# A fused attention and mixer kernel: batch 0's last casts off GpSimd, its mixed rows ahead of the turns, a mask and one v load moved

## The chip, the cores and the metric

The kernel runs on one core of one Trainium2 chip. The metric is the time of one execution on the device, in microseconds (us). A trace of one execution lies beside the times; its engines are TensorE (PE, with its weight loads as PEld), VectorE (DVE), ScalarE (ACT), GpSimd (POOL) and SyncE (SP).

## What is computed

Eight batches go through sparse attention and then through a mixer in tokens and channels. Cut to what matters:

```python
# q, k, v: (8 batches, 8 heads, 576 rows, 64); 8 global rows for all batches
scores = q @ k.T / 8
mask   = |i - j| <= 32  or  i is global  or  j is global
attn   = softmax(where(mask, scores, -1e9))
x      = concat_heads(attn @ v)                      # (8, 576, 512)
h      = relu(x.T @ w_tok1) @ w_tok2                 # 576 -> 256 -> 576
u      = x + h.T
out    = u + relu(u @ w_ch1) @ w_ch2                 # 512 -> 1536 -> 512
```

## The kernel before

**The tiles.** A batch's 576 rows are five tiles of 128 (tau, the last of 64 rows). Heads go in pairs p = 0 to 3. Loads bring q and k in f32 into `lq`, `lk` (rows 0 to 511) and `lr` (the 64 rest rows of both). These three buffers exist once, so a load for the next batch waits until the last one is cast. `cast_qk` (L365) makes f16 copies `qk` and `rn`. The rows must then be turned so that head elements lie on partitions. Batches 0 to 2 are turned on TensorE (`T`, `TR`) and copied out of PSUM into `qT`, `kT` by `TE` (L454) and `TR` (L458). Batches from 3 on are turned by DMA on SP's queue (`turns`, L752) and put in order by DVE (`order_*`).

**The attention.** `S_` makes the scores of a head pair in two PSUM tiles, and ACT takes their exponentials into `e_all` in three instructions (L494, L511, L516). For batch 0 the mask is added in the matmuls; for the others `SM` (L525) multiplies by `bandm` on DVE. `SM` also copies the columns of the global rows into `eg`. The scores of global rows go through `GK` (L540): two exponentials into `lf`, then a product with the 0/1 mask `mf`. `OG` (L562) multiplies `eg` by v. `PV` (L578) multiplies `e_all` by v, adds the product of `lf` with `OG`'s result `rf`, and divides by the sums into `x16`.

**The mixer.** `M1` and `M2` are the token part, its sums being `u16`. u is turned into `uT` by `M3` (L679), four DMA transposes on SP's queue (and one for the last 64 rows of two batches). `M4` (12 groups of four matmuls, relu by ACT or DVE) and `M5` are the channel part. Batch 0 has its own form: `M23_first` (L655) adds x and h for one tile, and `M3_first` (L671) turns that tile on TensorE and copies it out.

**The order** is written out by hand; each engine runs its instructions in the order of the program. After a prologue for batch 0 (L888 to L997), `period(b)` (L757) puts the channel part of batch b, held as a list `dense` from which `d(k)` takes k pieces, between the attention and the token part of batch b + 1. In period 0 (`n == 1`) these come one after another on GpSimd: `load_v16(2)` (L818, five DMAs that bring v of batch 2 and cast it to f16 into `vsh[0]`), four casts of k of batch 2, and `gather(1)` (four indirect DMAs). In the same period SP issues `load(3)` (q and k of batch 3; its lk waits for those four casts), the stores of batch 0 and the transposes of u of batch 1. In period 1 (`n == 2`) GpSimd casts batch 3: `casts(3)` (L808), first the rest rows, then eight pieces of q and k, then issues `load(4)` and `load_v16(3)`.

**PSUM.** Three buffers rotate under `s` (turned pieces, scores, `GK`, `OG`, `PV`, `pu`), two under `m` (`M4`, `M5` and others). A tile waits until the buffer three (or two) allocations back is read out.

The lines of the prologue that the change touches are L918 to L942 (casts, pads, turns and scores of batch 0) and L986 to L992 (mixed rows and turns of u of batch 0). In them `cast0(ti, p, eng)` casts head pair p of q (ti 0) or k (ti 1) of batch 0, `e_pads(i)` clears a part of `e_all` with a DVE memset (L190), `G0(p)` makes the global rows' part and `castv` casts v of batch 0 on GpSimd (L411).

Of the kernel before, what the change touches and what calls it, by code (L numbers as in the profile page):

```python
# [15 lines left out]
P = 128  # L16
NT = 5
# [9 lines left out]
def kernel(  # L27
# [12 lines left out]
    nc = tc.nc  # L40
# [148 lines left out]
    def e_pads(i):  # L189
        nc.vector.memset(  # L190
            (
                e_all[:, 2 * i : 2 * i + 2, :, 0:64] if i < NP else e_all[:, :, 0, 64:P] if i == NP
                else e_all[:, :, NT - 1, 64 + GW + P :]
            ), 0.0,
        )

    def row_numbers():
        nc.vector.tensor_scalar(out=idx_i, in0=bc_f, scalar1=hb, scalar2=gpp, op0=ALU.add, op1=ALU.add)
# [57 lines left out]
    def pads(i, eng):  # L256
        eng.memset(vsh[i][0:WIN, 0], 0.0)
        eng.memset(vsh[i][P - WIN : P, NT - 1], 0.0)
        eng.memset(vsh[i][:, :, :, D + 1 : VW], 0.0)
        eng.memset(vsh[i][:, :, :, D : D + 1], 1.0)  # L260
        eng.memset(x16s[i][LAST - 64 * i : P - 64 * i, NT - 1, :], 0.0)
# [4 lines left out]
    mf = const.tile([P, NT * P], F16)  # L266
# [88 lines left out]
    st = [dict() for _ in range(B)]  # L355

    def load_v16(b, c0=0, c1=NT):
        for c in range(c0, c1):
            r0, r1, j0 = vrows(c)
            nc.gpsimd.dma_start(  # L360
                out=vsh[b % 2][r0:r1, c, :, 0:D],
                in_=v[b, :, j0 : j0 + (r1 - r0), :].rearrange("h p d -> p h d"),
            )
# [9 lines left out]
    def casts(b, eng):  # L373
        return [lambda: cast_qk(b, 0, None, eng)] + [
            lambda ti=ti, p=p: cast_qk(b, ti, p, eng) for p in range(NP) for ti in range(2)
        ]
# [58 lines left out]
    def T(b, p):  # L435
        pT = pss([P, 2, 4 * P], F16, name=f"pT_{b}_{p}")
        for ti in range(2):
            for t in range(4):
                nc.tensor.transpose(out=pT[:, ti, P * t : P * t + P], in_=qk[:, ti, p, t], identity=ident)
        st[b]["pT", p] = pT  # L440
# [13 lines left out]
    def TE(b, p, copy):  # L454
        TE_q(b, p, copy)
        TE_k(b, p, copy)

    def TR(b, copy):  # L458
        pr = pss([P, NP, P], F16, name=f"pr_{b}")
        for p in range(NP):  # L460
            nc.tensor.transpose(out=pr[:, p], in_=rn[:, p], identity=ident)
        copy(out=qTs[b % 2][:, :, NT - 1, GW : GW + LAST], in_=pr[:, :, 0:LAST])
        copy(out=kTs[b % 2][:, :, WIN + 512 : WIN + S], in_=pr[:, :, LAST:P])
# [58 lines left out]
    def S_all(b, p):  # L522
        return S_(b, p, 0) + S_(b, p, 1)
# [16 lines left out]
    def GK(b):  # L540
        s = st[b]
        ps = pss([P, 2, 512], name=f"gk_{b}")
        for p in range(NP):
            o = ps[32 * p : 32 * p + 32]
            qv = qTs[b % 2][:, p, :, GW:QS]
            w = kgz[:, b, p, :]
            nc.tensor.matmul(o[:, 0, 0:384], lhsT=w, rhs=qv[:, 0:3], start=True, stop=True)
            nc.tensor.matmul(o[:, 1, 0:256], lhsT=w, rhs=qv[:, 3:5], start=True, stop=True)
        lf = mb.tile([P, NT * P], F16, tag="lf", name=f"lf_{b}")
        nc.scalar.activation(out=lf[:, 0:384], in_=ps[:, 0, 0:384], func=AF.Exp, scale=scale)  # L550
        nc.scalar.activation(out=lf[:, 384:640], in_=ps[:, 1, 0:256], func=AF.Exp, scale=scale)
        s["lf"] = lf
        if b > 0:
            nc.vector.tensor_mul(out=lf, in0=lf, in1=mf)
        else:
            lf_mask(0, 384)

    def lf_mask(x0, x1):
        lf = st[0]["lf"]
        nc.vector.tensor_mul(out=lf[:, x0:x1], in0=lf[:, x0:x1], in1=mf[:, x0:x1])  # L560

    def OG(b):  # L562
# [178 lines left out]
    def d(k, keep=0):  # L741
        for _ in range(k):
            if len(dense) > keep:
                dense.pop(0)()
# [12 lines left out]
    def period(b):  # L757
        n, m = b + 1, b + 2
        odd = b % 2
        dense.extend(lambda j=j: M4(b, j) for j in range(NJ))  # L760
        if odd:
            dense.extend(lambda j=j: M4l(b, j) for j in range(3))
        dense.extend(lambda t=t, i=i: M5(b, t, i) for t in range(4 + odd) for i in range(2))
        if n == B:
            d(len(dense))
            return
        tail = len(dense) - (23 if odd else 20) - 2 * odd
        keep = 3 if n == 1 else 0

        def scores(p, k):  # L770

            es = S_all(n, p)
            es[0]()
            es[1]()
            relu_on_dve[0] = n > 2 and p == 3
            d(1)
            relu_on_dve[0] = False
            es[2]()
            if n < 3 and p < 2:
                T(n, p + 2)  # L780
            d(1 + k)
            if n > 2 and p < 2:
                order(n, p + 2)
            if n < 3 and p < 2:
                TE(n, p + 2, dve)
            SM(n, p)

        if n == 1:
            d(1)
            gather_t(0)  # L790
            globals_(1)
            T(1, 1)
            TE_q(1, 1, act)
            TE_k(1, 1, dve)
            masks_d()
            pads(1, nc.vector)
            d(1)
            M2(0, 2)
        if n > 2:
            load(n + 2)  # L800
        scores(0, tail > 5)
        scores(1, max(tail - 4 - (tail > 5), 0))
        scores(2, 0)
        GK(n)
        if n > 2 and m < B:
            turns(m)
        if n == 2:
            for c in casts(3, nc.gpsimd.tensor_copy):  # L808
                c()
            load(4)  # L810
            turns(3)
        d(1)
        scores(3, 0)
        if n == 1:
            c2 = casts(2, nc.scalar.copy)
            for c in c2[0:1] + c2[1::2]:
                c()
            load_v16(2)  # L818
            for p in range(NP):
                cast_qk(2, 1, p, nc.gpsimd.tensor_copy)  # L820
            load(3, nc.sync)
            gather(1)
        d(1)
        OG(n)
        d(1)
        if n == 3:
            gather_t(1)
        fill = [order_rest, lambda i: order_k(i, 0), lambda i: order_q(i, 0), lambda i: order_k(i, 1), lambda i: order_q(i, 1)]
        lag = 2 if n == 1 else 1
        for tau in range(NT):  # L830
            PV(n, tau)
            if lag <= tau < 3 + lag:
                M1(n, tau - lag)
            if n > 2 and m < B:
                fill[tau](m)
            if n == 2 and tau > 2:
                fill[tau - 3](m)
            if tau < 4 and n > 1:
                d(1)
        if m < B:  # L840
            globals_(m)
        M1(n, 3)
        if n == 2:
            order_q(3, 0)
        d(1 if n == 1 else len(dense) - (8 + 2 * odd), keep)
        M1(n, 4)
        d(1, keep)
        if 2 < m < B:
            load_v16(m)
        M2(n, 0)  # L850
        M3(n, 0)
        M2(n, 1)
        M3(n, 1)
        M2(n, 2)
        if n % 2:
            M3(n, 2)
        if 1 < n < B - 2:
            for c in casts(n + 2, nc.scalar.copy):
                c()
        if n == 1:  # L860
            d(1, keep)
            T(2, 0)
            TE(2, 0, act)
            TR(2, dve)
            T(2, 1)
            d(1, keep)
            TE(2, 1, dve)
        else:
            d(1)
            if n == 2:  # L870
                order(3, 1)
                gather_c(1)
            d(1)

    act, dve = nc.scalar.copy, nc.vector.tensor_copy

    def exps(es):
        for x in es:
            x()

    def cast0(ti, p, eng):
        cast_qk(0, ti, p, eng)
# [32 lines left out]
    masks_l(NT - 1)  # L915
    masks_r(3)
    masks_l(3)
    for p in (2, 3):  # L918
        for ti in range(2):
            cast0(ti, p, nc.gpsimd.tensor_copy)  # L920
    w_pads()
    pads(0, nc.gpsimd)
    T(0, 1)
    TR(0, act)
    TE(0, 1, dve)
    exps(S_(0, 0, 1))
    e_pads(0)
    G0(1)
    T(0, 2)
    exps(S_all(0, 1))  # L930
    TE(0, 2, dve)
    G0(2)
    T(0, 3)
    exps(S_all(0, 2))
    TE(0, 3, dve)
    e_pads(1)
    G0(3)
    e_pads(2)
    row_numbers()
    e_pads(3)  # L940
    e_pads(4)
    exps(S_all(0, 3))  # L942
    SM(0, 0)
    SM(0, 1)
# [17 lines left out]
    load_wc2(4)  # L962
    GK(0)
    OG(0)
    lf_mask(384, NT * P)
    PV(0, 0)
    c1 = casts(1, act)
    for i in (0, 1, 3):
# [14 lines left out]
    for i in (2, 4):  # L983
        c1[i]()
    load(2)
    for tau in range(3):  # L986
        M23_first(tau)
    M3_first(0)
    M23_first(3)
    M3_first(1)  # L990
    M3_first(2)
    M3_first(3)  # L992
    TR(1, act)
    T(1, 0)
    TE_q(1, 0, act)
# [34 lines left out]
```

## Time and profile before

| | |
|---|---|
| median of 3 runs | 315.98 us (315.65 to 316.07) |
| the profiled execution | 316.27 us, of which the span of the trace is 314.2 us |
| PE | 299.7 us busy (95% of the span), 2588 matmuls |
| DVE | 193.8 us (62%) |
| ACT | 161.4 us (51%) |
| POOL | 81.1 us (26%) |
| HBM | 36.11 MB read, 9.44 MB written |

The 2.1 us between the execution's time and its span lie before the first and after the last recorded instruction. A span row of the timeline gives the start, the duration, the engine, the line, the operation with its tiles and count, and in brackets the idle time before it with what ended it. Several instructions of one kind are merged into one row. `POOL DMA_DIRECT2D` and `SPq DMA_...` rows are the issues of a DMA, not its transfer. q0 is the DMA queue that POOL issues to, q1 that of SP.

### The profile page before, as it was taken

What the parts mean: (1) busy time and instruction counts of PE and PEld (TensorE: products, weight loads), DVE (VectorE), ACT (ScalarE), POOL (GpSimd) and SP (SyncE); (2) the same over time, 40 slices, a digit from 0 to 9 for tenths busy, and PEclk for the clock granted to TensorE, in tenths of its full rate; (3) what the DMA queues carried; (4) which work ended last, traced back from release to release, by engine and by line L of the source; (5) the groups of instructions that cost most, each with busy time, mean ns of one, the idle gap of its engine ahead of it and who ended that gap; (6) DMA issues with size and microseconds to landing.
All of it is one profiled execution on the core that took longest, in us unless ns stands there. A gap on an engine that the chain in (4) does not pass through costs nothing.

```text
span 314.2 us, 6525 instructions
## 1 busy us (share of the span) xinstructions
PE 299.7 (95%) x2588; PEld 156.6 (50%) x2588; DVE 193.8 (62%) x425; ACT 161.4 (51%) x284; POOL 81.1 (26%) x127
## 2 busy tenths in 40 slices
PE   7979998996999999999999999999999999999993
PEld 3645545552466445544565445544574446444641
DVE  7877897676555678667874477577754585430021
ACT  5862882434737546485639464576533373205500
POOL 8898765458732001300140002200000000000000
PEclk9989999998999999999999999999999999999999
DMA  6999999999999999947993699945411420061022
GB/s 200 249 228 153 267 176 286 211 301 206 236 164 120 183 327 185 122 72 203 318 142 42 161 359 119 102 85 168 96 24 35 134 67 2 5 159 54 2 101 67
DMA packets 108512, 48.17 MB, mean 153 GB/s; under 512 B 87106, under 2 KB 102338, under 8 KB 108482
## 3 DMA queue, kind: packets, MB, share of 16 engines
q1 hardware_dynamic: 69712, 33.83, 47.2%
q0 software_dynamic: 38768, 13.93, 38.5%
q8 instruction: 20, 0.33, 0.4%
q14 instruction: 10, 0.08, 0.1%
q10 hardware_dynamic: 2, 0.00, 0.0%
HBM read 36.11 MB, written 9.44 MB: 145 GB/s over the span
## 4 chain that ended last, share of the span: by engine, by line
PE 86%; DVE 8%; ACT 3%; DMA 1%; issue 1%
PE op L728 29%; PE b1p L699 25%; PE a1p L620 5%; PE hp L644 5%; PE s L474 4%; PE b1lp L715 3%; PE pv L588 3%; PE pv L597 3%; PE pv L593 3%; DMA uT<-u 1%; DVE e_all L538 1%; PE og L567 1%; ACT e_all L494 1%; DVE kT L449 1%; PE idle L886 1%; DVE qT L443 1%
## 5 line engine op out<-in xcount | busy, mean ns | idle before, releaser
L699 PE MATMUL b1p<-uT,wc 128*128 128x512 f16 x384 | 95.6, 383 | 4.0 <-DMA uT<-u 2.6
L728 PE MATMUL op<-wc,b 128*128 128x512 f16 x384 | 88.1, 379 | 0.0
L705 ACT ACTIVATE b<-b1p 128x512 f16<-128x512 f32 x87 | 52.3, 601 | 65.0 <-PE b1p L699 60.5
L699 PEld LDWEIGHTS <-wc 128*128 128x128 f16 x384 | 35.2, 98 | 46.6 <-issue 6.4
L728 PEld LDWEIGHTS <-b 128*128 128x128 f16 x384 | 36.3, 98 | 43.4
L360 POOL DMA_DIRECT2D vsh<-in_v_dram x35 | 30.3, 878 | 100.5 <-PE pv L597 94.1
L732 DVE TENSOR_TENSOR osb<-u,op 128x512 f32<-128x512 f16 x32 | 21.9, 686 | 47.0 <-PE op L728 46.9
L494 ACT ACTIVATE e_all<-s 128x832 f16<-128x832 f32 x32 | 27.6, 864 | 41.7 <-issue 31.3
L538 DVE TENSOR_TENSOR e_all<-e_all,bandm 128x1040 f16<-128x1040 f16 x56 | 37.4, 708 | 1.0
L650 DVE TENSOR_TENSOR u<-x,hp 128x512 f16<-128x512 f16 x28 | 17.4, 681 | 23.0 <-PE hp L644 23.0
L605 DVE TENSOR_TENSOR x<-pv,rr 128x512 f16<-128x512 f32 (+1 forms) x40 | 27.6, 691 | 1.4
L588 PEld LDWEIGHTS <-e_all 128*128 128x128 f16 x320 | 21.7, 100 | 5.6 <-DVE x L605 0.5
L588 PE MATMUL pv<-vsh,e_all 128*128 128x66 f16 x320 | 24.0, 196 | 0.0
L511 ACT ACTIVATE e_all<-s 128x576 f16<-128x576 f32 x32 | 20.8, 651 | 0.4 <-PE s L474 0.4
L593 PE MATMUL pv<-vsh,e_all 128*128 128x66 f16 x256 | 20.7, 197 | 0.0
L604 DVE RECIPROCAL rr<-pv 128x8 f32<-128x8 f32 (+1 forms) x40 | 8.2, 206 | 20.2 <-PE pv L597 19.9
L474 PE MATMUL s<-qT,kT 64*128 64x208 f16 (+1 forms) x320 | 19.4, 244 | 0.1
L593 PEld LDWEIGHTS <-e_all 128*128 128x128 f16 x256 | 17.6, 100 | 3.1
L620 PE MATMUL a1p<-x,w 128*128 128x512 f16 x64 | 18.7, 379 | 0.0
L474 PEld LDWEIGHTS <-kT 64*128 64x128 f16 x320 | 11.3, 95 | 14.6 <-issue 12.9
L516 ACT ACTIVATE e_all<-s 128x416 f16<-128x416 f32 x32 | 17.0, 530 | 0.0
L644 PE MATMUL hp<-a,w 128*128 128x512 f16 x72 | 16.8, 378 | 0.0
(180 smaller groups left out, 346.0 us busy)
## 6 DMA issues: line engine op xcount, KB each, us to landing
out_dram<-osb SPq DMA_DIRECT2D x32, 256.0 KB, 2.3
lq<-in_q_dram SPq DMA_DIRECT2D x4, 1024.0 KB, 6.6
lk<-in_k_dram SPq DMA_DIRECT2D x4, 1024.0 KB, 9.1
wc<-in_moe_w_ch_dram POOLq DMA_DIRECT2D x6, 512.0 KB, 9.5
vsh<-in_v_dram POOLq DMA_DIRECT2D x21, 128.0 KB, 8.6
lq<-in_q_dram POOLq DMA_DIRECT2D x2, 1024.0 KB, 9.0
lk<-in_k_dram POOLq DMA_DIRECT2D x2, 1024.0 KB, 12.6
vsh<-in_v_dram POOLq DMA_DIRECT2D x14, 96.0 KB, 8.3
```

The source lines that it names most:

```text
L360: nc.gpsimd.dma_start(out=vsh[b % 2][r0:r1, c, :, 0:D], in_=v[b, :, j0 : j0 + (r1 - r0), :].rearrange("h p d -> p h d"),)
L474: nc.tensor.matmul(ps[:, par, off : off + n], lhsT=kT[r, P * c : P * c + P], rhs=qf[r, lo : lo + n], start=b > 0, stop=b > 0 or c > 1 and ...
L494: nc.scalar.activation(out=e2[:, :, 1:3, 64:EW], in_=ps[:, :, 0 : 2 * W].rearrange("p h (c x) -> p h c x", c=2), func=AF.Exp, scale=scale,)
L538: nc.vector.tensor_mul(out=eh, in0=eh, in1=bandm)
L588: nc.tensor.matmul(o, lhsT=e_all[:, h, tau, EW - P - sh : EW - sh], rhs=vsh[b % 2][:, tau, h, :], start=hh == 0, stop=False,)
L593: nc.tensor.matmul(o, lhsT=e_all[:, h, tau + 1, 0:P], rhs=vsh[b % 2][:, tau + 1, h, :], start=False, stop=False)
L605: nc.vector.tensor_tensor(out=x16s[b % 2][r, tau, :].rearrange("p (f h x) -> p f h x", f=2, h=NP), in0=pq[r, :, :, 0:D], in1=rr[r].unsquee ...
L620: nc.tensor.matmul(ps[tt], lhsT=w, rhs=x16s[b % 2][:, ch, :], start=(ch == 0), stop=(ch == NT - 1))
L644: nc.tensor.matmul(ps[:, i, :], lhsT=w2[:, ch, P * tau - sh : P * tau - sh + P], rhs=s["a1"][:, ch, :], start=(ch == 0), stop=(ch == 1),)
L699: nc.tensor.matmul(ps, lhsT=wc1[:, cc, P * j : P * j + P], rhs=s["uT"][:, cc, :], start=(cc == 0), stop=(cc == 3))
L705: nc.scalar.activation(out=s["b1"][:, j, :], in_=ps, func=AF.Relu)
L728: nc.tensor.matmul(ps, lhsT=w, rhs=wc2[:, j, :], start=(j == 0), stop=(j == NJ - 1))
```

## The change

Four things are changed; the work that is computed stays the same.

1. In the prologue the f16 casts of head pairs 2 and 3 of batch 0 go from POOL to ACT (pair 2) and DVE (pair 3). The copy behind `TR(0)` goes from ACT to DVE. The memsets `e_pads` are put at other places of DVE's order.
2. The mixed rows of batch 0: all four `M23_first` run ahead of all four `M3_first`.
3. The mask of the global weights `lf`, for batches from 1 on, is multiplied after the next piece of the channel part instead of straight behind the exponentials.
4. `load_v16(2)` is issued from the end of period 0, behind the cast of batch 3's rest rows, instead of ahead of the casts of k of batch 2. That cast of the rest rows goes along from the head of `casts(3)` in period 1.

```diff
         s["lf"] = lf
-        if b > 0:
-            nc.vector.tensor_mul(out=lf, in0=lf, in1=mf)
-        else:
-            lf_mask(0, 384)
-
-    def lf_mask(x0, x1):
-        lf = st[0]["lf"]
+        if b == 0:
+            lf_mask(0, 0, 384)
+
+    def lf_mask(b, x0=0, x1=NT * P):
+        lf = st[b]["lf"]
         nc.vector.tensor_mul(out=lf[:, x0:x1], in0=lf[:, x0:x1], in1=mf[:, x0:x1])
...
         if n == 2:
-            for c in casts(3, nc.gpsimd.tensor_copy):
+            for c in casts(3, nc.gpsimd.tensor_copy)[1:]:
                 c()
             load(4)
             turns(3)
         d(1)
+        lf_mask(n)
         scores(3, 0)
         if n == 1:
             c2 = casts(2, nc.scalar.copy)
             for c in c2[0:1] + c2[1::2]:
                 c()
-            load_v16(2)
             for p in range(NP):
                 cast_qk(2, 1, p, nc.gpsimd.tensor_copy)
             load(3, nc.sync)
...
             d(1, keep)
             TE(2, 1, dve)
+            casts(3, nc.gpsimd.tensor_copy)[0]()
+            load_v16(2)
...
-    for p in (2, 3):
-        for ti in range(2):
-            cast0(ti, p, nc.gpsimd.tensor_copy)
+    e_pads(0)
+    e_pads(1)
     w_pads()
     pads(0, nc.gpsimd)
+    cast0(0, 2, act)
+    cast0(1, 2, act)
     T(0, 1)
-    TR(0, act)
+    TR(0, dve)
     TE(0, 1, dve)
     exps(S_(0, 0, 1))
-    e_pads(0)
     G0(1)
+    cast0(0, 3, dve)
+    cast0(1, 3, dve)
     T(0, 2)
     exps(S_all(0, 1))
     TE(0, 2, dve)
     G0(2)
+    e_pads(2)
     T(0, 3)
     exps(S_all(0, 2))
     TE(0, 3, dve)
-    e_pads(1)
-    G0(3)
-    e_pads(2)
-    row_numbers()
     e_pads(3)
     e_pads(4)
+    G0(3)
+    row_numbers()
...
-    for tau in range(3):
+    for tau in range(NT - 1):
         M23_first(tau)
-    M3_first(0)
-    M23_first(3)
-    M3_first(1)
-    M3_first(2)
-    M3_first(3)
+    for tau in range(NT - 1):
+        M3_first(tau)
```

More of the change, by code (lines that the diff above doesn't have):

```diff
@@ L964 @@
     OG(0)
-    lf_mask(384, NT * P)
+    lf_mask(0, 384)
     PV(0, 0)
```

## The prediction

> **What bounds the kernel now.** First the page: the busy times and the chain that ended last.
>
> ```profile
> PE 299.7 (95%) x2588; PEld 156.6 (50%) x2588; DVE 193.8 (62%) x425; ACT 161.4 (51%) x284; POOL 81.1 (26%) x127
> PE 86%; DVE 8%; ACT 3%; DMA 1%; issue 1%
> ```
>
> PE is busy for 95%, and 86% of the chain is PE. So a gain must come out of the 14.5 us in which PE idles (span 314.2 us), or out of time at a lower granted clock. Second, PE's waits, longest first (us in total, times, longest); third, the stretches around the two longest. The column behind the busy times is the granted clock, then DMA share and GB/s.
>
> ```profile
> PE b1p L699 <- DMA uT<-u: 2.6, 1, 2.6
> PE og L567 <- DVE eg L528: 1.8, 2, 1.6
> ...
> PE b1p L699 <- DVE b L703: 1.0, 1, 1.0
> ```
>
> ```profile
> 17.60:21.00 3.40, 1.37 (x39) 0.84 (x32) 3.01 (x13) 2.90 (x7) 3.35 (x7) 1.00 1.04 319
> 21.00:24.40 3.40, 3.34 (x49) 2.86 (x46) 2.45 (x6) 0.24 (x1) 2.79 (x4) 0.50 1.18 146
> 72.20:75.60 3.40, 0.82 (x10) 0.43 (x7) 3.37 (x6) 0.18 (x1) 3.40 (x6) 1.00 1.30 249
> 75.60:79.00 3.40, 3.40 (x17) 1.18 (x16) 0.61 (x1) 1.89 (x3) 3.40 (x6) 0.50 0.92 250
> 79.00:314.20 235.20, 230.09 (x1897) 118.26 (x1895) 133.34 (x265) 117.84 (x208) 22.59 (x27) 1.00 0.75 128
> ```
>
> Two places matter. At 17.6 to 21.0 PE works 1.37 of 3.4 us, and at 72.2 to 75.6 0.82; each time the clock of the next 3.4 us is 0.50, which costs 1.7 us of work once more. From 79 us PE is busy 230.1 of 235.2 us: whatever is gained ahead of 75 us reaches the end. And the second place filters the first:
>
> ```profile
> 71.93 0.61 PE L439 MATMUL pT<-ident,qk 128*128 128x128 f16 x8
> 75.12 1.41 PE L699 MATMUL b1p<-uT,wc 128*128 128x512 f16 x4 [2.58 <-DMA uT<-u]
> ```
>
> PE is through at 72.54 and starts M4 of batch 1 at 75.12, when its uT has landed. A PE that comes there earlier only waits longer. **The end moves as uT's landing moves**, down to the moment at which PE is ready.
>
> **Parts 1 to 3: when PE is ready.** The rows around OG of batch 0, in the chain and among the groups:
>
> ```profile
> 18.04 0.41 ACT e_all L516
> ...
> 20.10 0.13 DVE eg L528
> ...
> 20.27 0.48 PE og L567 x17
> ```
>
> ```profile
> 12.33 0.61 POOL L371 CAST qk<-lk 128x512 f16<-128x512 f32 x1
> ...
> 18.00 1.72 POOL L411 CAST vsh<-lv 128x512 f16<-128x512 f32 x3
> ```
>
> ```profile
> L462 DVE COPY qT<-pr x1: 283/283/283, 65.2 to 65.2; 128x256 f16<-128x256 f16 x1
> L411 DVE CAST vsh<-lv x1: 403/403/403, 19.7 to 19.7; 96x512 f16<-96x512 f32 x1
> ```
>
> POOL loses four casts of 0.61, the last of which is shown, so its casts of v end not at 19.72 but at 17.3 or earlier, and its later issues move up by about as much. DVE gets two copies (2 x 0.28) and two casts (2 x 0.40, by the nearest row), 1.36 us. T(0,2) reuses the PSUM buffer that TE(0,1) reads, so of the 1.36 us the 0.56 of the copies put off the scores of pairs 1 and 2, by about 0.45 us on ACT's chain of exponentials. That chain ends at 18.45 and would end near 18.9. The two memsets moved ahead and one moved behind take DVE's queue off the end: the last eg can follow the last exponential by its 0.2 us, so OG runs at 19.2 instead of 20.27. I take a gain of 1.0; bounds -0.5 (a DVE as full as now, plus the 0.45) and 1.5 (ACT not put off). PE's idle time between 17.6 and 21.0 falls from 2.0 to 1.0 us; if that keeps the clock, up to 1.7 more come; I take 0.8, between the ends, since no row shows a stretch of about 70% busy.
>
> ```profile
> 30.55 0.22 PE pu L675 x4
> ...
> 47.34 0.40 DVE lf L554
> 47.74 0.61 DVE b L703
> ```
>
> Part 2 takes the turns of tile 0 (0.22) from ahead of tile 3's rows, on which the chain goes on: 0.2; bounds -0.6 (pu of tile 2 now waits for the buffer that an ACT copy of 0.58 reads) and 0.4. Part 3 takes lf's 0.40 from ahead of the relu that PE waits for (the 1.0 above): 0.4; in later periods ACT makes those relus, and the mask is due only at PV: 0. **PE is ready at 72.54 - 1.0 - 0.8 - 0.2 - 0.4 = 70.1**, between 68.9 and 73.0.
>
> **Part 4: when uT lands.** The queues that it stands in, by POOL's and SP's rows:
>
> ```profile
> 51.13 1.65 POOL L360 DMA_DIRECT2D vsh<-in_v_dram  x2 [0.61 <-PE og L567]
> 59.31 2.28 POOL L371 CAST qk<-lk 128x512 f16<-128x512 f32 x4 [6.54 <-DMA lk<-in_k_dram]
> ...
> 66.59 0.62 POOL L368 CAST rn<-lr 128x512 f16<-128x512 f32 x1
> ...
> 71.70 0.64 POOL L371 CAST qk<-lk 128x512 f16<-128x512 f32 x1 [3.72 <-DMA lk<-in_k_dram]
> ```
>
> ```profile
> 61.62 0.37 SPq L86 DMA_DIRECT2D lk<-in_k_dram  x1
> 62.09 0.92 SPq L733 DMA_DIRECT2D out_dram<-osb  x1
> 63.12 8.97 SPq L686 DMA_TRANSPOSE uT<-u  x4
> ```
>
> The transposes are issued from 63.12, behind lk of batch 3, which lands at 71.70. The DMA queues, first for 60 to 62 us, then for 72 to 75 us (packets, MB, share):
>
> ```profile
> q0 software_dynamic: 2281, 0.29, 225.3%
> q1 hardware_dynamic: 69, 0.04, 8.7%
> ```
>
> ```profile
> q1 hardware_dynamic: 2242, 0.62, 128.4%
> ```
>
> ```profile
> 70.00:72.00 2.00, 2.00 (x19) 1.02 (x19) 1.83 (x4) 1.43 (x3) 0.30 (x1) 1.00 0.61 45
> ```
>
> Between 60 and 62 q0 moves v of batch 2 (576 rows x 8 heads = 4608 packets) at 1140 packets a us, while q1, where lq of batch 3 has waited since its issue, moves 69. With v gone q1 wins those 2 us and some of the stretch before it, in which both share: 2 to 3.5 us; I take 3.0. lk must not hold that back: it needs POOL's casts of k of batch 2 to end by about 61 (61.59 now), and POOL's lead and a q0 without v's tail give them about 1 us. The transposes then begin to move at 66 instead of about 69.
>
> But v comes back right there. POOL's order becomes casts of k, gathers, rn, five v issues, then the casts of batch 3. With rn 1 us earlier (65.6 to 66.2) the five issues (0.83 each) stand at 66.2 to 70.4, packets some 2 us behind them: 68.2 to 72.4. What is queued behind them on POOL, eight casts of 0.6, today waits 3.72 us for lk anyway, so these end about as now (76.7), and load(4) with them: 0. OG of batch 2, which needs v, runs at 84.85 now: 8 us of cover even after a gain of 4.
>
> Today the transposes take 6 us, 69 to 75, of which 70 to 72 moves hardly anything (45 GB/s). From 66, 2.2 us pass freely; about 1.2 of the lull fall under v's start; the last 2.6 us of work go at half pace beside v until 72.4 and freely after it: 73.0. The ends: 71.5 with v wholly under the lull or 3.5 us won, 76 and more with q1 shut out for v's whole 4 us. The half pace is my choice; 60 to 62 shows worse.
>
> The Trainium skill ("DMA: Bandwidth & Descriptors", Queues, rings and completion order) says that each DMA engine goes round-robin between the queues with work, a packet at a time. By that rule v and the transposes share, as I took it, and 73.0 stands; by the row of 60 to 62 they do not, and 76 comes nearer. The rule speaks against putting v beside the transposes, whichever queue issues it.
>
> **The sum.** PE goes on at max(70.1, 73.0 + 0.1) = 73.1 instead of 75.12: -2.0. The gap is 3.0 us, so the drop of the clock behind it stays. 316.27 - 2.0 = 314.2; the profiled execution was 0.29 above the median of 315.98, so 313.9 stands against the runs; I give **313.8**.
>
> **The rivals.** *A, v hides and the clock stays.* uT lands at 71 to 72 with PE ready at 70, the gap is 1 to 2 us, and of the 1.7 us of clock some or all is spared: -3.1 to -5.8, so 310.2 to 312.9. For it: the lull at 70 to 72, and SP's transposes issued long before. Against it: the 2.58 gap now drops the clock to 0.50. The Trainium skill ("TensorE: Matmul & The Clock Gate", HAM oscillation) warns of gaps above about 3.4 us; the trace disagrees, since 2.58 us was enough here. By the page's figure neither gap would cost clock.
>
> *B, v's return eats it all.* v shares worse than half and uT lands near 75; parts 1 to 3 only lengthen the wait: 315.3 to 316.6. For it: the same bytes pass the same DMA before uT as now.
>
> *C, slower: q1 shut out.* If v's first packet passes before the first transposes have left, q1 stands still as at 60 to 62 for v's 4 us, and 5 to 6 us of transposes follow: 72.4 + 5 = 77.4, PE 2.3 us later than now, 318.3 (316.6 to 319). It decides at lk's landing: once lk of batch 3 drains after 68, C holds.
>
> *D, the change doesn't do what it says*: lk(2)'s landing, not v, holds q1, and lk(3) is issued at 61.6 as now. Then lq is won but lk is not, the transposes start at 67 to 68: B's times.
>
> **How the numbers follow.** Forecast (312.9 to 315.3) 0.45; A 0.27; B with D 0.12; C 0.16. A measurement of this kernel can tell about 0.2%, 0.63 us, from no change. So faster 0.72, same 0.12, slower 0.16. 310.4 to 316.9 leaves out a quarter of A and most of C, about 0.2.
>
> **What would show it.** OG of batch 0 at 19.2 with a clock of 1.00 after it; the relu of group 8 ahead of lf's mask and a PE wait there of 0.6; lk of batch 3 landing near 68.5; M4 of batch 1 starting at 73. It is wrong if lk lands after 70, if uT lands after 75, or if PE shows a wait for v at OG of batch 2 or for wc at M4 of batch 0, where loads now come earlier than they are cast.

## The result, and the profile after

The changed kernel takes 314.05 us (median of 20 runs, 312.29 to 315.92) beside 315.68 us for the kernel before (20 runs, 313.65 to 319.02). The ratio is 0.9959 with a 95% interval of 0.9939 to 0.9978: faster by 1.3 us (0.7 to 1.9). The forecast was 313.8. **The number was right, most of its cause was not, and that the two agree is in part luck:** part 4, on which it rested, brings nothing and seems to cost time, and part 1 brings it, by a path that the prediction priced far too low.

The profiled execution took 313.5 us with a span of 311.5. The busy times and the end of the chain of waits on its page, against 299.7 us and 86% of PE before:

```profile
PE 298.0 (96%) x2588; PEld 155.6 (50%) x2588; DVE 196.3 (63%) x429; ACT 162.1 (52%) x284; POOL 78.3 (25%) x123
PE 84%; DVE 7%; ACT 3%; DMA 2%; SPq 2%; issue 1%; DVEq 0%
```

PE's longest waits, in us in total, times, longest:

```profile
PE idle L886 <- DVE wz L114: 1.2, 1, 1.2
PE a1p L618 <- DVE x L603: 0.9, 3, 0.5
PE b1p L697 <- DVE osb L730: 0.8, 1, 0.8
PE og L565 <- DVE eg L528: 0.8, 2, 0.4
PE b1p L697 <- DVE b L701: 0.6, 1, 0.6
```

(Lines behind the change stand two lower than before: L699 is now L697.) The wait for uT, 2.58 us before, is not there. One for osb is, which was not there before: osb is the sum of u and the channel part that VectorE makes for the output, and M4 takes over the PSUM buffer that this sum reads. The relu wait (b) went from 1.0 to 0.6. The stretches that were shown of before, now of after; the column behind the five busy times is the granted clock:

```profile
17.60:21.00 3.40, 2.38 (x60) 1.62 (x55) 2.86 (x13) 2.58 (x6) 3.10 (x5) 1.00 1.19 279
21.00:24.40 3.40, 2.67 (x53) 2.01 (x50) 1.76 (x4) 1.14 (x2) 2.49 (x4) 1.00 1.23 252
24.40:27.80 3.40, 2.10 (x15) 0.97 (x15) 1.75 (x5) 0.00 (x0) 3.12 (x4) 1.00 1.11 178
72.20:75.60 3.40, 2.56 (x26) 1.43 (x25) 3.37 (x5) 2.29 (x5) 3.40 (x5) 1.00 1.73 241
75.60:79.00 3.40, 3.40 (x30) 1.38 (x28) 3.33 (x8) 2.91 (x7) 3.40 (x6) 1.00 0.81 193
```

Both halvings of the clock are gone. But PE is busy only 2.67 and 2.10 us of the two stretches behind 21.0, where before it had been busy for 3.34 and 3.26, the first of them at half clock. The timeline of PE shows why little came of the earlier OG:

```profile
19.28 0.46 PE L565 MATMUL og<-vsh,eg 128*32 128x132 f16 x17 [0.39 <-DVE eg L528]
...
23.73 0.19 PE L591 MATMUL pv<-vsh,e_all 128*128 128x66 f16 x1 [0.42 <-issue]
24.47 0.27 PE L595 MATMUL pv<-rf,lf 128*128 128x264 f16 x1 [0.38 <-issue]
25.90 0.36 PE L586 MATMUL pv<-vsh,e_all 128*128 128x66 f16 x6 [0.52 <-issue]
...
29.69 1.12 PE L659 MATMUL hp<-a,w 128*128 128x512 f16 x4 [0.47 <-ACT a L623]
```

OG stands at 19.28 (forecast 19.2), 1 us earlier than before. Then come three stops of 1.3 us together to which the profile gives no releaser ("issue"), and `M23_first`, which began at 28.78 before, begins at 29.69. So PE reaches M4 of batch 1 at 73.03, not at 70.1.

**A second profile of each kernel** was taken (314.18 us after, 316.81 us before). The changed kernel then took another way to nearly the same time; first PE's rows, then the two stretches around the wait:

```profile
19.22 0.46 PE L565 MATMUL og<-vsh,eg 128*32 128x132 f16 x17 [0.38 <-DVE eg L528]
...
26.45 1.12 PE L659 MATMUL hp<-a,w 128*128 128x512 f16 x4 [0.47 <-ACT a L623]
...
73.10 1.86 PE L697 MATMUL b1p<-uT,wc 128*128 128x512 f16 x4 [2.83 <-DMA uT<-u]
```

```profile
72.20:75.60 3.40, 2.50 (x14) 0.99 (x14) 2.05 (x3) 0.55 (x2) 3.40 (x5) 0.63 1.78 214
75.60:79.00 3.40, 3.40 (x24) 1.21 (x20) 0.76 (x2) 3.17 (x8) 3.40 (x5) 0.87 1.24 293
```

No stops this time: `M23_first` begins at 26.45, PE is through at 70.27 (forecast 70.1), waits 2.83 us for uT, starts M4 at 73.10 (forecast 73.1), and pays for the gap with its clock. This is the forecast's own path. The kernel before, in its second profile, again waits for uT:

```profile
PE b1p L699 <- DMA uT<-u: 2.4, 1, 2.4
```

Every profile can be laid out by the same five numbers: when `M23_first` begins, when PE is ready for M4 of batch 1, when uT has landed (the last of its four transposes), when M4 begins, and how long it then is to the end of the span.

| kernel | profiled us | M23_first | PE ready | uT landed | M4 of batch 1 | from there |
|---|---|---|---|---|---|---|
| before | 316.27 | 28.78 | 72.54 | 75.0 | 75.12 | 239.1 |
| before, second | 316.81 | 28.80 | 72.53 | 74.8 | 74.97 | 239.9 |
| after | 313.50 | 29.69 | 73.03 | 72.0 | 73.03 | 238.5 |
| after, second | 314.18 | 26.45 | 70.27 | 73.0 | 73.10 | 239.1 |
| p4_alone | 317.69 | 30.75 | 76.03 | 76.5 | 76.66 | 238.9 |
| p1_alone | 314.25 | 29.50 | 74.25 | 73.2 | 74.25 | 238.0 |
| p23 | 315.98 | 31.86 | 76.36 | 75.5 | 76.36 | 237.7 |
| p234 | 317.07 | 31.80 | 76.11 | 75.9 | 76.11 | 238.9 |
| p123 | 316.62 | 32.19 | 76.88 | 74.1 | 76.88 | 237.7 |
| p123_again | 312.70 | 29.23 | 72.34 | 73.0 | 73.09 | 237.7 |
| no_v | 312.17 | 29.35 | 72.38 | 69.1 | 72.38 | 238.0 |
| v_last | 318.41 | 29.68 | 72.92 | 70.3 | 72.92 | 243.5 |
| v_mid | 314.92 | 26.10 | 70.01 | 71.5 | 71.65 | 241.3 |
| shift24 | 309.89 | 26.66 | 69.88 | 70.0 | 70.17 | 237.7 |

The last column is 237.7 to 238.0 where nothing disturbs it. A halved clock behind a long wait for uT adds 1.4 to 2.2, a wait for osb 0.8 to 1.2, and a wait for v (v_last, v_mid) 3.6 or more. M4 begins at the later of "PE ready" and uT. One profile of a kernel may lie anywhere in its spread, so what follows compares medians first and uses profiles for the mechanism.

### The profile page after: what moved, and what is told of

Same layout as the page of the kernel before. It is cut to its first block, busy times and chain, and to the rows that moved or that the text cites. A ratio compares the mean times of both kernels' runs of the same rounds, so it can differ in the third digit from the quotient of the medians.

```text
span 311.5 us, 6526 instructions
## 1 busy us (share of the span) xinstructions
PE 298.0 (96%) x2588; PEld 155.6 (50%) x2588; DVE 196.3 (63%) x429; ACT 162.1 (52%) x284; POOL 78.3 (25%) x123
## 4 chain that ended last, share of the span: by engine, by line
PE 84%; DVE 7%; ACT 3%; DMA 2%; SPq 2%; issue 1%; DVEq 0%
PE op L726 30%; PE b1p L697 25%; PE a1p L618 5%; PE hp L642 5%; PE s L474 4%; PE b1lp L713 3%; PE pv L595 3%; PE pv L586 3%; PE pv L591 2%; DMA lk<-in_k_dram 2%; DVE e_all L538 2%; DVE kT L449 1%; SPq L86 1%; PE og L565 1%; ACT e_all L494 1%; DVE qT L443 1%
## 5 line engine op out<-in xcount | busy, mean ns | idle before, releaser
L697 PE MATMUL b1p<-uT,wc 128*128 128x512 f16 x384 | 94.4, 380 | 1.8 <-DVE osb L730 0.8
L726 PEld LDWEIGHTS <-b 128*128 128x128 f16 x384 | 36.4, 98 | 43.4
L697 PEld LDWEIGHTS <-wc 128*128 128x128 f16 x384 | 35.1, 98 | 43.5 <-issue 5.4
L586 PEld LDWEIGHTS <-e_all 128*128 128x128 f16 x320 | 21.0, 97 | 6.8 <-issue 1.3
L586 PE MATMUL pv<-vsh,e_all 128*128 128x66 f16 x320 | 23.7, 193 | 0.5 <-issue 0.5
L602 DVE RECIPROCAL rr<-pv 128x8 f32<-128x8 f32 (+1 forms) x40 | 8.2, 206 | 20.9 <-PE pv L595 20.2
L591 PE MATMUL pv<-vsh,e_all 128*128 128x66 f16 x256 | 20.0, 193 | 0.4 <-issue 0.4
L591 PEld LDWEIGHTS <-e_all 128*128 128x128 f16 x256 | 16.7, 97 | 3.1
L371 ACT CAST qk<-lq 128x512 f16<-128x512 f32 x25 | 15.0, 616 | 4.0 <-DMA lq<-in_q_dram 4.0
```

Of the source, the lines that this page charges most:

```text
L586: nc.tensor.matmul(o, lhsT=e_all[:, h, tau, EW - P - sh : EW - sh], rhs=vsh[b % 2][:, tau, h, :], start=hh == 0, stop=False,)
L591: nc.tensor.matmul(o, lhsT=e_all[:, h, tau + 1, 0:P], rhs=vsh[b % 2][:, tau + 1, h, :], start=False, stop=False)
L697: nc.tensor.matmul(ps, lhsT=wc1[:, cc, P * j : P * j + P], rhs=s["uT"][:, cc, :], start=(cc == 0), stop=(cc == 3))
L726: nc.tensor.matmul(ps, lhsT=w, rhs=wc2[:, j, :], start=(j == 0), stop=(j == NJ - 1))
```

## The experiments

Each ratio is to the kernel before, timed beside it on the same chip. Three groups ran on three chips: p4_alone to no_v, p1_alone to v_last, v_mid to after_again; the kernel before took 315.98, 315.90 and 316.42 us there.

### p4_alone: part 4 on the kernel before

```diff
-            for c in casts(3, nc.gpsimd.tensor_copy):
+            for c in casts(3, nc.gpsimd.tensor_copy)[1:]:
...
-            load_v16(2)
...
+            casts(3, nc.gpsimd.tensor_copy)[0]()
+            load_v16(2)
```

> Part 4 alone in the kernel before (v of batch 2 and the cast of batch 3's rest rows at the end of period 0; prologue, mixed rows and mask as before). Theory 1, the end follows the landing of uT: uT lands at 71 to 73 instead of 75.0, PE is ready at 72.5 as before, so the 2.58 us wait at M4 of batch 1 falls under 0.6, the drop of the clock behind it goes, and the kernel is 1.5 to 4 us faster than before (312 to 314.5). Theory 2, the gain comes from the prologue: the same as before within 0.6 us.

Measured: 316.84 us (12 runs, 315.49 to 319.19), ratio 1.0023 (0.9998 to 1.0048). Part 4, which was to bring the whole 2 us, brings nothing and may cost 0.7 us. In its profile PE waits 0.63 us for uT and 0.57 us for osb. uT lands there at 76.5, later than before; but `M23_first` is 2 us later too and SP issues the transposes of uT only from 65.6 (63.1 before), so this profile alone doesn't tell what part 4 does to uT.

### p123: the changed kernel without part 4

```diff
+            load_v16(2)
             for p in range(NP):
                 cast_qk(2, 1, p, nc.gpsimd.tensor_copy)
...
-            casts(3, nc.gpsimd.tensor_copy)[0]()
-            load_v16(2)
```

> The changed kernel without part 4 (v of batch 2 issued where it was before). Theory 1: PE still waits for uT at M4 of batch 1, which lands at 74 to 75.5, and the time stays within 0.8 us of before. Theory 2: 1 us or more faster than before, with the same wait for uT shorter than 2 us or gone.

Measured: 312.93 us (6 runs), ratio 0.9891 (0.9858 to 0.9925). It is faster than the changed kernel, by 1.1 us in the medians and 2.1 by the ratios. Its profiled execution, 316.62 us, was the slowest of the six, with a wait of 1.62 us for rf at 21.88 and the clock at half behind it, which is why p123_again was run.

### p234: the changed kernel without part 1

```diff
+    for p in (2, 3):
+        for ti in range(2):
+            cast0(ti, p, nc.gpsimd.tensor_copy)
...
-    cast0(0, 2, act)
-    cast0(1, 2, act)
...
-    TR(0, dve)
+    TR(0, act)
...
-    cast0(0, 3, dve)
-    cast0(1, 3, dve)
```

> The changed kernel without part 1 (prologue's casts, copies and memsets as before; mixed rows, mask and v as changed). If part 1 only moves the moment at which PE is ready and loses what it won at OG between 21 and 27 us, this is as fast as the changed kernel or up to 1 us faster (312 to 314). If part 1 is needed for the gain (the DMAs that POOL issues 2.5 us earlier), uT lands later than 73 and it is 1 us or more slower than the changed kernel.

Measured: 315.71 us (12 runs), ratio 1.0008 (0.9979 to 1.0036). Without part 1 nothing of the gain is left that these runs can tell. In its profile PE waits 1.4 us for osb.

### no_v: the changed kernel with v of batch 2 not loaded

The five DMAs of v of batch 2 are left out, so batch 2 is computed with the v that stands in that buffer.

```diff
             casts(3, nc.gpsimd.tensor_copy)[0]()
-            load_v16(2)
```

> The changed kernel with the load of v of batch 2 left out, so that batch 2 is multiplied by v of batch 0. If v beside the transposes costs nothing (v's packets come when the transposes are nearly done), within 0.6 us of the changed kernel. If v at its new place still holds uT or what follows up, 1.5 us or more faster than the changed kernel.

Measured: 312.91 us (6 runs), ratio 0.9898 (0.9863 to 0.9933). With v gone altogether the kernel is no faster than p123, in which v is loaded at its old place. So v at the old place costs nothing that these runs can tell, and v at the new place 1 to 2 us. M4 of batch 1 starts at 72.38 without a wait, and osb is not waited for. But v does hold uT, as the trace's account of the four transposes shows (when the first and the last were issued, and how long they took to land), here and in p123_again, which has v at the old place:

```profile
L684 SPq DMA_TRANSPOSE uT<-u x4: 1211/1279/1747, 62.1 to 66.6; - x4
DMA to landing us min/median/max: 2.5/4.0/5.6
```

```profile
L684 SPq DMA_TRANSPOSE uT<-u x4: 1322/1410/2411, 61.9 to 67.3; - x4
DMA to landing us min/median/max: 5.6/5.6/5.6
```

Without v the last transpose lands 2.5 us behind its issue, at 69.1; with v at the old place 5.6 us behind it, at 72.95. The 3.9 us do not show in the time, because PE is not ready before 72.38. With v at the new place uT lands at 72.0 and 73.0.

### p1_alone and p23: the other parts on the kernel before

The first has the lines of p234's edit the other way round and the pads of `e_all` moved, the second parts 2 and 3 of the diff.

> The kernel before with part 1 alone (casts of pairs 2 and 3, TR's copy and the pads of the prologue). Theory 'prologue' (what is gained ahead of 30 us reaches the end, since the uT wait of the one profile of before is not typical): as much as the runs without part 1 showed it to be worth, 315.7 - 314.0 = 1.7 us, so 314.0 to 314.6. Theory 'filter' (the prediction's: PE only waits longer for uT of batch 1 until part 4 lets it land earlier): within 0.5 us of the kernel before, 315.5 to 316.5, with a PE wait for uT of 3 us or more in the profile.

> The kernel before with parts 2 and 3 alone (mixed rows ahead of the turns; global weights masked later). Theory 'prologue': the rest of what parts 1 to 3 gained together, 3.0 - 1.7 = 1.3 us, so about 314.7 (314.4 to 315.4). Theory 'filter': 315.5 to 316.5. A third: the two groups help only together, because each of them alone runs into the next wait (OG's eg for parts 2 and 3, x or u for part 1): both kernels above 315 although p123 stood at 312.9.

Measured: p1_alone 313.59 us (12 runs), ratio 0.9931 (0.9901 to 0.9962); p23 315.50 us (12 runs), ratio 0.9985 (0.9960 to 1.0010). Part 1 alone makes 2.2 us (1.2 to 3.1), where the whole change makes 1.3 (0.7 to 1.9); parts 2 and 3 make 0.5 us, which is not told from nothing. The "filter" theory, by which part 1 alone changes nothing, falls. The three sums, -2.2, -0.5 and +0.7, give -2.0 beside the -1.3 measured, within their intervals.

### p123_again: a second profile without part 4

The kernel is that of p123.

> Parts 1 to 3 without part 4 once more, for a second profile and a second time: 312.9 again (312.3 to 313.4). In its profile by the theory 'GpSimd under VectorE' (v's five issues put the casts of batch 3 under VectorE's products of the first head pair of batch 2): eg 0.23 us and e_all 2 x 0.7 there, since the casts run ahead and then wait for the turns of the pairs before, and a PE wait for osb under 0.3 us. By the rival 'uT': a PE wait for uT of 0.5 us or more at the start of the channel part of batch 1, and no gain from taking part 4 back.

Measured: 313.29 us (7 runs), ratio 0.9913 (0.9879 to 0.9947), profiled at 312.70. Here lies the answer. PE's row at M4 of batch 1:

```profile
73.09 1.02 PE L697 MATMUL b1p<-uT,wc 128*128 128x512 f16 x4 [0.75 <-DMA uT<-u]
```

The wait for uT is there, as the rival said, and it ends at 73.09: 2.03 us earlier than before, with v of batch 2 at its **old** place. PE itself is no earlier than before (72.34 against 72.54). So the whole gain up to there is uT's, and part 4 had no hand in it. Behind it 1.4 us more are won, because after the shorter wait the clock isn't halved (237.7 instead of 239.1). GpSimd's timelines show where uT's lead comes from; first before, then p123_again:

```profile
21.46 0.76 POOL L229 DMA_DIRECT2D wc<-in_moe_w_ch_dram  x1
...
46.63 0.89 POOL L86 DMA_DIRECT2D lk<-in_k_dram  x1
```

```profile
18.52 0.78 POOL L229 DMA_DIRECT2D wc<-in_moe_w_ch_dram  x1
...
44.22 0.89 POOL L86 DMA_DIRECT2D lk<-in_k_dram  x1
...
56.01 2.29 POOL L371 CAST qk<-lk 128x512 f16<-128x512 f32 x4 [5.74 <-DMA lk<-in_k_dram]
...
68.24 0.62 POOL L371 CAST qk<-lk 128x512 f16<-128x512 f32 x1 [2.54 <-DMA lk<-in_k_dram]
```

Without its four casts GpSimd issues the first channel weights 2.9 us earlier. Everything that it loads after them stands in the same queue: lk of batch 2 is issued 2.4 us earlier, its casts begin at 56.01 instead of 59.31, and so lk of batch 3, which waits for these casts and stands ahead of the transposes, lands by 68.24 instead of 71.70. The same row for the first weights is at 18.0 to 19.7 in all nine profiles with part 1 and at 20.9 to 22.1 in all five without it; that of lk of batch 2 at 43.4 to 45.9 and at 46.1 to 47.6. A rival is that u is ready earlier, so that its transposes are issued earlier: here they are, by 1.2 us. In p1_alone they are issued 0.9 us later than before (64.0 against 63.1), and uT still lands 1.8 us earlier (73.2 against 75.0). So it is the queue ahead of them that has moved. No run moves GpSimd's four casts without the other edits of part 1; that these casts do it is read from the rows. As to the GpSimd theory, eg took 0.54 and the two e_all products 1.60 us, a little over the 0.23 and 1.31 expected, without a wait for osb.

### v_last and v_mid: what part 4 costs

```diff
             casts(3, nc.gpsimd.tensor_copy)[0]()
-            load_v16(2)
...
                 c()
+            load_v16(2)
             load(4)
```

> The changed kernel, with v of batch 2 issued behind all nine casts of batch 3 instead of ahead of eight of them. Theory 'GpSimd under VectorE': the casts run from about 66.5 us, wait for the turns, and miss VectorE's products; eg 0.23 us, no PE wait for osb over 0.3, so 1 us of part 4's cost goes: 313.0 (312.5 to 313.4). Rival 'traffic' (v's packets in these microseconds cost, wherever they stand): 314.0 as the changed kernel. Rival 'cover': v is issued at 74 to 78 us and lands only near 80 to 82, PE waits for v at OG of batch 2: 314 to 316, with that wait in the profile.

Measured: 318.98 us (8 runs), ratio 1.0088 (1.0051 to 1.0125). The third expectation came true and was larger than thought: v is issued at 74.11 to 78.43, beside the transposes of q and k of batch 3, and OG of batch 2 waits twice:

```profile
PE og L565 <- DMA vsh<-in_v_dram: 3.7, 2, 2.8
```

The time is therefore no verdict on the first theory, but the rows ahead of OG are. VectorE's timeline of the changed kernel and what GpSimd did meanwhile, then VectorE's of v_last:

```profile
70.94 1.75 DVE L532 TENSOR_TENSOR eg<-e_all,bandm 128x160 f16<-128x160 f16 x1
72.72 2.01 DVE L538 TENSOR_TENSOR e_all<-e_all,bandm 128x1040 f16<-128x1040 f16 x2
74.66 0.68 DVE L730 TENSOR_TENSOR osb<-u,op 128x512 f32<-128x512 f16 x1
```

```profile
66.54 4.32 POOL L360 DMA_DIRECT2D vsh<-in_v_dram  x5
70.80 0.68 POOL L371 CAST qk<-lq 128x512 f16<-128x512 f32 x1
...
73.11 1.07 POOL L371 CAST qk<-lq 128x512 f16<-128x512 f32 x1
74.14 1.07 POOL L371 CAST qk<-lk 128x512 f16<-128x512 f32 x1
```

```profile
70.83 0.23 DVE L532 TENSOR_TENSOR eg<-e_all,bandm 128x160 f16<-128x160 f16 x1
71.10 1.31 DVE L538 TENSOR_TENSOR e_all<-e_all,bandm 128x1040 f16<-128x1040 f16 x2
72.67 0.69 DVE L730 TENSOR_TENSOR osb<-u,op 128x512 f32<-128x512 f16 x1 [0.26 <-PE op L726]
```

In the changed kernel v's issues hold GpSimd until 70.86, and its eight casts begin as VectorE's products do. A product of 0.23 us takes 1.75, two of 1.31 take 2.01, osb's sum comes 2 us later, and PE waits 0.84 us for it (75.39 instead of 74.38 for the second group of M4). In v_last the casts are over at that time and the wait is gone. p4_alone and p234, in which v has its new place too, repeat it: 1.16 and 1.15 us for the product, 3.13 and 3.12 for the two. In after's second profile the product took only 0.52 us. The Trainium skill ("SBUF — State Buffer", Who interferes with whom) says that a VectorE instruction with two inputs in SBUF contends with a GpSimd instruction that reads SBUF, for a shared port pair that works as an exclusive lock. The 0.23 against 1.75 us, and casts of 1.07 instead of 0.6, agree.

```diff
-            casts(3, nc.gpsimd.tensor_copy)[0]()
+            for c in casts(3, nc.gpsimd.tensor_copy)[0:5]:
+                c()
             load_v16(2)
...
-            for c in casts(3, nc.gpsimd.tensor_copy)[1:]:
+            for c in casts(3, nc.gpsimd.tensor_copy)[5:]:
```

> The changed kernel, with the first four casts of q and k of batch 3 put ahead of the five issues of v of batch 2, the last four left behind them. The four run at about 66.5 to 69 us, v is issued at 69 to 73.3, so nothing of GpSimd's casts lies under VectorE's products of the first head pair (70.3 to 71.9), and v lands by about 77, ahead of OG at 81. Theory 'GpSimd under VectorE': no PE wait for osb over 0.3 us, no wait for v, 313.0 (312.5 to 313.4), 1 us under the changed kernel; the last casts may fall under the second pair's products, behind which no PE work waits. Rival 'traffic': v's packets, later than in the changed kernel, cost as much: 314.0. Rival 'cover': a wait for v at OG of batch 2 as in v_last (3.7 us there): 315 or more.

Measured: 312.59 us (6 runs, 309.70 to 314.92), ratio 0.9844 (0.9795 to 0.9894). The median lies where the first theory put it. The ratio says more than that theory can give: 4.9 us less than the kernel before, where the changed kernel has 1.3. The one run of the changed kernel on this chip took 314.18, 1.6 us more than this median; how much of the rest is the chip's is not shown. Its profiled execution was the slowest of the six and apart from the others, so its rows tell of that one: no wait for osb, but 1.41 us for v at OG, since the first lk of batch 3 came only at 68.03 and held the casts, and v behind them:

```profile
68.03 1.17 POOL L371 CAST qk<-lk 128x512 f16<-128x512 f32 x1 [2.29 <-DMA lk<-in_k_dram]
...
70.72 4.32 POOL L360 DMA_DIRECT2D vsh<-in_v_dram  x5
```

```profile
71.72 2.06 DVE L538 TENSOR_TENSOR e_all<-e_all,bandm 128x1040 f16<-128x1040 f16 x2
```

The last row shows that casts are not the whole of it: the two products took 2.06 us instead of 1.31 while GpSimd had only v's issues on hand (70.72 to 75.04). So the order mends the wait for osb and stands at the edge of the one for v.

### shift24: what the stops at 23 to 26 us hang on

```diff
-    fill(2)
+    for _ in range(26):
+        nc.tensor.matmul(idle[:, 0:8], lhsT=wz[:, 0:P], rhs=wz[:, 0:8], start=True, stop=True)
     masks_a1()
```

> The changed kernel, with the two filling matmuls of 512 columns ahead of the first turns replaced by 26 of 8 columns: 24 more matmuls on PE ahead of everything, in about the same 1 us. It tells what PE's unexplained gaps at 23 to 26 us hang on (matmuls 263 to 272 of the program in the profile of the changed kernel). Theory 'supply' (PE runs out of instructions, which are fetched 16 KB at a time): the gaps come at the same count, 256 to 280, and so 24 matmuls earlier in the program, in the second tile of PV instead of the third, about 0.7 us earlier; the fetch recorded at 24.2 moves with them. Theory 'data' (something that the third tile of PV needs arrives late): the gaps stay at the same matmul of the program, count 287 to 296. Time: within 0.5 us of the changed kernel by both, 313.5 to 314.5.

Measured: 310.36 us (6 runs, 309.84 to 311.54), ratio 0.9809 (0.9765 to 0.9852): 6 us less than the kernel before, the fastest of all, and expected by neither theory. Its question was not answered: the stops do not occur in its profile at all, at either place. `M23_first` begins at 26.66, and uT lands at 70.0, 2 to 3 us earlier than in the changed kernel:

```profile
70.17 1.02 PE L697 MATMUL b1p<-uT,wc 128*128 128x512 f16 x4 [0.29 <-DMA uT<-u]
```

### before_again and after_again

> The kernel before, for a second profile: was the uT wait of 2.58 us in its first profile typical? Theory 'filter': 2 us or more again. Theory 'prologue': under 1 us, with M23_first of batch 0 starting 1 to 2 us later than the 28.78 of the first profile, and the clock at half twice ahead of 36 us.

> The changed kernel, for a second profile. What recurs in both is taken as its own: by the theories so far OG of batch 0 at 19.2 to 19.4 with the clock at 1.00 behind it, gaps of PE without a releaser at 23 to 26 us, an eg product of over 1 us at 71 and a PE wait for osb of 0.5 us or more; no uT wait over 0.5.

Measured: 316.81 and 314.18 us; their rows stand in the first section. Before: 2.44 us for uT, `M23_first` at 28.80. So the wait is that kernel's own, and my theory that the first profile was not typical falls. After: OG at 19.2 and the clock behind it recur; the stops, the wait for osb and the absence of a wait for uT do not. Nor does the long product (0.52 us). PE's wait for uT until 73.10 covers whatever VectorE is late by.

## Why the prediction was right, and where it was not

- **The bound held.** PE starts M4 of batch 1 at the later of its own readiness and uT's landing; both profiles of before wait there (2.58, 2.44). A PE that came 2.8 us earlier only waited longer: the second profile of after is 0.7 us slower than the first.
- **OG at 19.2 with the clock kept: right** (19.28 and 19.22, clock 1.00 in both). Part 3's 0.4 too: b's wait went from 1.0 to 0.6. Parts 2 and 3 were given 0.6 together; p23 shows 0.5 with an interval that holds 0. No wait for v at OG of batch 2 nor for wc at M4 of batch 0 came up in the changed kernel.
- **PE ready at 70.1: 70.27 in one profile, 73.03 in the other.** The working held where PE met no stops; the stops, 1.3 us of "issue" and what they put off behind them, were in no term. Their cause was not found.
- **uT at 73.0: the number held (72.0 and 73.0 in the two profiles), two of its terms did not.** That q1 gains when v is gone was right, and by more than the 3.0 that I took: 3.9 us (69.1 in no_v against 73.0 in p123_again). But v's return beside the transposes takes 2.9 to 3.9 us of that back, where the half pace gave 1.0. So part 4, on top of part 1, moves uT by 0 to 1 us, not by 2.0. What moved it was a clause of part 1, "its later issues move up by about as much", to which I gave "about 1 us" and which I used only as cover for lk of batch 2. It is worth 1.8 to 2.0 us at uT (73.2 in p1_alone and 73.0 in p123_again against 75.0). That what was missing in one term stood in the other is luck.
- **"Parts 1 to 3 only lengthen the wait" (rival B) failed for the same reason:** p1_alone gains 2.2 us.
- **v beside the transposes: sharing was right, its price was not.** In the changed kernel the two queues did share, from 68 to 70 us:

```profile
q1 hardware_dynamic: 796, 0.19, 72.2%
q0 software_dynamic: 786, 0.10, 90.7%
```

  Besides the 2.9 to 3.9 us at uT, a price came where I had written "end about as now: 0". Casts of batch 3 that had waited for lk now ran as one block under VectorE's products. I had asked when they end, not what runs beside them.
- **Of rival A a part came true.** In the first profile uT landed at 72.0 and the clock stayed, but PE came only at 73.03.
- **Rival C did not occur** (no M4 after 73.1 in the changed kernel). lk of batch 3 landed at 66.9 in its second profile, earlier than the 68.5 that I gave. Of rival D one half held. GpSimd's and SyncE's rows of the changed kernel:

```profile
57.62 2.29 POOL L371 CAST qk<-lk 128x512 f16<-128x512 f32 x4 [10.87 <-DMA lk<-in_k_dram]
```

```profile
59.94 0.37 SPq L86 DMA_DIRECT2D lk<-in_k_dram  x1
```

  lk of batch 3 is issued right behind the casts of k of batch 2 (57.62 + 2.29 = 59.91), and these wait for their own lk; v's absence doesn't release them.
- **The 313.8** stood because -2.0 was put on the right wait, though on the wrong part. By the runs the changed kernel's gain is part 1's 2.2 us less what part 4 costs (0.7 on the kernel before, where it is not told from nothing; 1 to 2 on top of the other parts). With its own terms the sum is 314.0 (316.27 - 2.0 - 0.29), not 313.8.

**Open:** the stops ahead of 30 us, and why shift24 is faster by so much. In its profile both things go well at once, no stops and uT at 70.17. No stops were seen either in the other profiles of the changed order on that chip (v_mid and after_again), so it may be the chip; its early uT, which the 1 us lead of lk of batch 2 over after_again (43.80 against 44.77) explains in part, was seen once. That the 26 small matmuls cause it is not shown.

## What to carry to other kernels

Follow a moved instruction's whole queue: by the rows here, four casts of 0.6 us taken off the engine that issues the loads moved a landing 50 us later by 2 us, and the part of the diff with these casts was worth more than the other parts. When a wait sits between two streams, ask of every part of the change what it does to both, and test each part alone, since a right total can hide a part that costs. A run with one load left out tells what it holds up only if no other wait stands behind it: look at the landing, too, and not only at the time. When a block of instructions changes its time, check what runs beside it on an engine that it can slow, not only when it ends.

## What the runs showed of the hardware

- **When the clock is halved.** A wait of 0.75 us (p123_again) and one of 1.64 us (v_mid) at M4 of batch 1 left the clock at 1.00; 2.44 us (before, second) brought 0.63 in the next stretch. In v_mid it was halved only at 82.30, behind a wait for v of 1.41 us. Its rows, in stretches of 3.41 us laid so that the halved one stands alone:

```profile
68.64:72.05 3.41, 1.77 (x15) 0.95 (x13) 3.38 (x7) 1.21 (x3) 3.41 (x5) 1.00 1.24 250
72.05:75.46 3.41, 3.41 (x30) 1.40 (x29) 1.73 (x2) 2.70 (x6) 3.41 (x5) 1.00 1.41 221
78.88:82.30 3.42, 1.74 (x25) 0.73 (x25) 1.55 (x3) 1.60 (x4) 3.42 (x5) 1.00 1.64 157
82.30:85.71 3.41, 3.41 (x27) 1.91 (x24) 0.89 (x2) 0.60 (x1) 2.83 (x4) 0.50 1.29 175
```

  A stretch with 1.77 us busy, which holds the single wait of 1.64, kept the clock; one with 1.74 in which no wait was over 1.41 lost it. 2.10 us busy kept it in after (24.4 to 27.8). So it looks like the share of a stretch, about a half, rather than one long gap. It is no sharp limit in these traces: 1.86 us busy lost the clock in before's second profile (18.45 to 21.86).
- **An engine can stop without a releaser.** Between 23 and 29 us, with the DMA engines loaded at 1.1 to 1.2, PE stopped for 0.2 to 1.2 us at a time in six of the nine profiles with part 1 (up to 2.1 us together) and in p234 of those without. In p4_alone VectorE stood idle for 1.34 us and began a reciprocal at 27.88, though the last product that it could wait for had ended at 26.40. Such time is as large as the effect of the whole change.
